# A retention and serf kernel on one core: k transposed on VectorE as q is, both from squares rearranged in DRAM

## Chip, cores and metric

The kernel runs on one core of one Trainium2 chip. The metric is the device time in microseconds (us) of one execution. The core has five engines that work at the same time, each through its own queue of instructions in order: TensorE (PE, with its weight loads as PEld), VectorE (DVE), ScalarE (ACT), GpSimd (POOL) and SyncE (SP), which here issues nearly all transfers. Sixteen DMA engines carry the transfers.

## The reference

Two blocks follow each other, all in float32. First comes retention, an attention without softmax: q, k and v have 8 batches of 8 heads with 576 positions of 64 values.

```python
scores = (1.0 / np.sqrt(D)) * np.matmul(q, k.transpose(0, 1, 3, 2))
gamma = 1.0 - 2.0 ** (-5.0 - np.arange(H))
rel = pos[:, None] - pos[None, :]
Dmat = np.where(rel >= 0, gamma[:, None, None] ** rel, 0.0)
x = np.matmul(scores * Dmat, v)          # then (B, H, S, D) -> (B*S, H*D): 4608 x 512
```

Then a feed-forward block with w_in (512 x 2048) and w_out (2048 x 512):

```python
h = x @ w_in
sp = np.maximum(h, 0.0) + np.log1p(np.exp(-np.abs(h)))
out = (h * erf(sp)) @ w_out
```

## The kernel before

**Attention by pieces.** A batch's 576 positions are cut into four pieces of 128 and one of 64, 40 pieces in all, numbered on through the batches. Each piece passes three stages. `transposes(i)` starts the loads of piece i + 3, weighs the values of piece i + 1 on GpSimd with decay powers gk (L276, in place in raw_v) and makes qT and kT, with two heads in the 128 partitions. `scores(i)` multiplies kT with qT (L311) and masks on VectorE (sT). `outputs(i)` forms o from sT and v (L323), adds the state of the pieces before (L334), makes the new state from kv (L346), and writes o, times its decay, into x (L376). The stages come in the fixed order transposes(i + 1), outputs(i), scores(i + 1). Because decay powers count from the start of the batch, the state is a plain sum: one copy on ScalarE (L358) or additions on VectorE; x takes one operation for each pair of heads, with a scalar gs by piece and a table gq.

**Two ways to transpose.** In batches 0 and 1, q and k go through TensorE against an identity (L296, into pt_q and pt_k) and are copied out by ScalarE (L297). VectorE transposes 32 x 32 squares only within themselves. From batch 2 on (`SQUARES = 2`), `load_squares(b)` fetches q of a whole batch in four transfers (L125) that bring every 32 x 32 square to the partitions where its transpose belongs, in runs of 32 values (128 B); VectorE then makes qT in one operation per piece (L299). k still goes through TensorE in all batches.

**Loads.** `load` fetches k and v (L115, four buffers each), and in the first two batches q (two buffers), each in two transfers with rows of 64 values (256 B). SP issues them in program order: an issue that waits for its buffer holds back all behind it.

**Feed-forward.** The 4608 positions are taken in 9 chunks of 512 (`TCH`), the hidden width in 4 groups. A `First` block multiplies x with w_in (L432) and a `Second` block the result with w_out (L511), each as seven products in a Strassen-like scheme, with sums on VectorE (the helper `tt`, L92) and copies, softplus and erf on ScalarE. In group 0 the steps of attention for later chunks are set between the products by hand: `attend(upto)` issues stages up to a mark, and `run(steps, rounds, stages)` calls it before each product. The operands of x are stored to DRAM (xd, L420) and read again for groups 1 to 3; partial outputs go to od (L567).

**Weights.** Each weight arrives as 64-bit words (wraw, three buffers, L200) and is rounded to float32 in steps: two operations on ScalarE (L217, L218), four on VectorE (L222 to L235), two on GpSimd (L236, L237), after which the next weight is fetched; four sums follow at the end of a set. `round_weights(n)` issues n such steps. In the first attention pieces, two steps follow each stage from the second on:

```python
    while done[0] < stages_for(TCH):
        attend(done[0] + 1)
        if done[0] >= 2:
            round_weights(2)
```

Of the kernel before, what the change touches and what calls it, by code (L numbers as in the profile page):

```python
# [11 lines left out]
FP32 = mybir.dt.float32  # L12
# [7 lines left out]
B, H, S, D = 8, 8, 576, 64  # L20
D_MODEL, D_FF = 512, 2048
NP = H // 2
NS = -(-S // P)
CONST_COLS = NS * H + NP * P + NS * NP + P

# [4 lines left out]
def decays():  # L32


    gamma = 1.0 - 2.0 ** (-5.0 - np.arange(H, dtype=np.float64))
    pairs = gamma.reshape(2, NP)
    t = np.arange(P)
    starts = np.arange(NS) * P
    gk = pairs.T.reshape(1, 1, H) ** -(starts[None, :, None] + t[:, None, None])
    row = pairs.repeat(D, axis=0)  # L40
    gq = row[:, :, None] ** t[None, None, :] / math.sqrt(D)
    gs = row[:, None, :] ** starts[None, :, None]
    tri = t[None, :] >= t[:, None]
    return np.concatenate([x.reshape(P, -1) for x in (gk, gq, gs, tri)], axis=1).astype(np.float32)


@with_exitstack
def kernel(
# [25 lines left out]
    dram = ctx.enter_context(tc.tile_pool(name="dram", bufs=n_ch, space=bass.MemoryType.DRAM))  # L74
    cpool = ctx.enter_context(tc.tile_pool(name="cpool", bufs=1))
    wpool = ctx.enter_context(tc.tile_pool(name="wpool", bufs=2))
    wraw = ctx.enter_context(tc.tile_pool(name="wraw", bufs=3))
    raw = ctx.enter_context(tc.tile_pool(name="raw", bufs=4))
    att = ctx.enter_context(tc.tile_pool(name="att", bufs=2))
    xpool = ctx.enter_context(tc.tile_pool(name="xpool", bufs=2))  # L80
# [15 lines left out]


    pieces = [(b, s0, min(P, S - s0)) for b in range(B) for s0 in range(0, S, P)]
    loaded = {i: {} for i in range(len(pieces))}


    SQUARES = 2
    SQ = 32

    def load(i, names="kv"):
        if i >= len(pieces):
            return
        b, s0, n = pieces[i]
        for name, src in (("q", q), ("k", k), ("v", v)):
            if name in names and not (name == "q" and b >= SQUARES):  # L110
                bufs = 2 if name == "q" else 4
                t = raw.tile([P, H, D], FP32, tag=name, name=f"raw_{name}", bufs=bufs)
                for e in range(2):
                    heads = src[b, e * NP : (e + 1) * NP, s0 : s0 + n, :]
                    nc.sync.dma_start(out=t[:n, e::2, :], in_=heads.rearrange("h p d -> p h d"))  # L115
                loaded[i][name] = t

    squares = {}

    def load_squares(b):  # L120
        if SQUARES <= b < B:
            t = squares[b] = raw.tile([P, NP, S // SQ, SQ], FP32, tag="q4", name="raw_q4", bufs=2)
            for part in range(P // SQ):
                e, d0 = part // 2, part % 2 * SQ
                nc.sync.dma_start(  # L125
                    out=t[part * SQ : (part + 1) * SQ].rearrange("r p a d -> r (p a) d"),
                    in_=q[b, e * NP : (e + 1) * NP, :, d0 : d0 + SQ].rearrange("p (a r) d -> r (p a) d", r=SQ),
                )

    load(0, "qkv")  # L130
    cst = cpool.tile([P, CONST_COLS], FP32, name="cst")
    nc.scalar.dma_start(out=cst, in_=consts)
    ends = [0]
    for m in (NS * H, NP * P, NS * NP, P):
        ends.append(ends[-1] + m)
    gk, gq, gs, tri = (cst[:, a:b] for a, b in zip(ends, ends[1:]))
    gk = gk.rearrange("p (s h) -> p s h", s=NS)
    gq = gq.rearrange("p (a i) -> p a i", a=NP)
    load(1, "qkv")
    load(2)  # L140


# [97 lines left out]
            if sums:  # L240
                yield from sums(*(w[:, i] for i in range(7)))

    for _ in range(3):
        load_weights()
    round_step = rounding()

# [23 lines left out]

    def weigh_values(i):

        if i < len(pieces):
            _, s0, n = pieces[i]
            t = loaded[i]["v"]
            nc.gpsimd.tensor_tensor(  # L276
                out=t[:n],
                in0=t[:n],
                in1=gk[:n, s0 // P, :].unsqueeze(2).to_broadcast([n, H, D]),
                op=ALU.mult,  # L280
            )

    def transposes(i):
        b, s0, n = pieces[i]
        t = live[i] = loaded.pop(i)
        load(i + 3)
        load(i + 2, "q")
        if s0 == 0:
            load_squares(b + 1)
        weigh_values(i + 1)  # L290
        for name in "qk":
            tT = t[name + "T"] = att.tile([P, NP, P], FP32, tag=name + "T", name=name + "T")
            if name in t:
                pt = ps_at.tile([P, NP, P], FP32, tag="at", name=f"pt_{name}")
                for p in range(NP):
                    nc.tensor.transpose(pt[:, p, :n], flat(t[name][:n, 2 * p : 2 * p + 2, :]), ident[:n, :n])  # L296
                nc.scalar.copy(out=tT[:, :, :n], in_=pt[:, :, :n])  # L297
            else:
                nc.vector.transpose(  # L299
                    out=tT[:, :, :n].rearrange("p a (s i) -> p a s i", i=SQ),  # L300
                    in_=squares[b][:, :, s0 // SQ : (s0 + n) // SQ, :],
                )

    def scores(i):
        n, t = pieces[i][2], live[i]
# [11 lines left out]
    def outputs(i):  # L317
# [24 lines left out]
        if s0 + n < S:  # L342
            kv = ps_at.tile([P, NP, D], FP32, tag="at", name="kv")
            for p in range(NP):
                for e in range(2):
                    nc.tensor.matmul(  # L346
                        kv[e * D : (e + 1) * D, p, :],
                        lhsT=t["k"][:n, 2 * p + e, :],
                        rhs=t["v"][:n, 2 * p + e, :],
                        start=(p == 0),  # L350
                        stop=(p == NP - 1),
                        skip_group_check=True,
                    )
            old = kept.get("state")
            if pieces[i + 1][2] > D:
                new = att.tile([P, NP, D], FP32, tag="state", name="state")
                if s0 == 0:
                    nc.scalar.copy(out=new, in_=kv)  # L358
                else:
                    tt(new, kv, old, ALU.add)  # L360
            else:
                new = states[b % 2]
                for r in heads:
                    tt(new[r, :, r], kv[r], old[r], ALU.add)
            kept["state"] = new
        t0 = b * S + s0
        while t0 < b * S + s0 + n:
            c = t0 // TCH
            if (0, c) not in x:
                x[0, c] = x_tile()  # L370
            m = min(b * S + s0 + n, (c + 1) * TCH) - t0
            a = t0 - b * S - s0
            at = slice(t0 - c * TCH, t0 - c * TCH + m)
            for p in range(NP):
                j = s0 // P * NP + p
                nc.vector.scalar_tensor_tensor(  # L376
                    out=x[0, c][:, p, at],
                    in0=o[:, p, a : a + m],
                    scalar=gs[:, j : j + 1],
                    in1=gq[:, p, a : a + m],  # L380
                    op0=ALU.mult,
                    op1=ALU.mult,
                )
            t0 += m

    stages = [(transposes, 0), (scores, 0)]
# [196 lines left out]
    weigh_values(0)  # L583
    while done[0] < stages_for(TCH):
        attend(done[0] + 1)
        if done[0] >= 2:
            round_weights(2)
    operands_x(0, 0)


# [2 lines left out]
    def run(steps, rounds=(), stages=1):  # L593

        for step, _ in enumerate(steps):
            attend(min(done[0] + stages, most[0]))
            if step in rounds:
                round_weights()

    run(firsts[0].first(), (0, 1), 2)  # L600
    run(firsts[0].middle(), (0, 1, 2), 2)
    run(firsts[0].last(), (0, 1), 2)
    firsts[0].erf()
    most[0] = stages_for(3 * TCH) - 1
    attend(stages_for(2 * TCH))
    operands_x(0, 1)
    round_weights(4)
    run(firsts[1].first(), (0, 1))
    firsts[0].multiply()
    round_weights(4)  # L610
    for b, nxt in zip(blocks[1:], blocks[2:] + [None]):
        n = order.index((b.g, b.c))
        if isinstance(b, First):
            most_g[0] = order[n - 1][0] + 1
            seconds[n - 1].begin()
            if n + 1 < n_s and order[n + 1][0] > 0:
                load_x(*order[n + 1])
            run(b.middle(), (0, 1))
            firsts[n - 1].sums()
            if n == 1:  # L620
                round_weights(9)
            run(seconds[n - 1].first(), (0, 1))
            run(b.last())
            most[0] = stages_for(min((n + 3) * TCH, n_tok)) - (n + 3 < n_ch)
        elif n + 2 < n_s:
            f = firsts[n + 1]
            for step, _ in enumerate(b.middle()):
                attend(min(done[0] + 1, most[0]))
                if step == 0:
                    f.erf()  # L630
            if n + 2 < n_ch:
                attend(stages_for((n + 3) * TCH))
            operands_x(*order[n + 2])
            run(nxt.first(), (0,))
            f.multiply()
            run(b.last(), (1,))
        elif n + 1 < n_s:
            firsts[n + 1].erf()
            seconds[n + 1].begin()
            run(b.middle())  # L640
            run(b.last())
            firsts[n + 1].multiply()
            firsts[n + 1].sums()
            run(nxt.first())
        else:
            run(b.middle())
            run(b.last())
# [30 lines left out]
```

## Time and profile before

| | |
|---|---|
| Median of three runs | 1090.24 us (1087.63 to 1090.39) |
| Profiled execution, its own time | 1091.13 us |
| Its span, first to last instruction | 1089.4 us |
| Mean granted TensorE clock | 0.987 |
| DMA moved | 178.60 MB in 170376 packets, 144448 of them under 512 B |
| Last copy of kT (piece 39) begins | 369.5 us |

A profile is one execution. The busy share of an engine is an average over stages with different limits, so the windows by stage say more than the page's sums. A line such as "A L1 <- B L2: us, times, longest" means that engine A stood idle before line 1 until line 2's work on B was done. A row of windows gives, for a stretch of the span, the busy time and number of instructions of PE, PEld, DVE, ACT and POOL, then the granted TensorE clock, the busy share of the DMA engines (packets can overlap, so it can pass 1) and the GB/s moved.

### The profile page before, as it was taken

Reading aid. Unit: us, or ns where it says so; the run is one execution under the profiler, and the core shown is the slowest. Engines: PE = TensorE matmul, PEld = TensorE weight load, DVE = VectorE, ACT = ScalarE, POOL = GpSimd, SP = SyncE. Lnnn points to the kernel's source line nnn. Section 1 sums busy time; section 2 is a strip of 40 time slices with the busy share of each in tenths; the row PEclk is TensorE's granted clock in tenths of the full one; section 3 lists DMA queues with packets and bytes.
Section 4 is the critical chain, followed back from the end, with each engine's and each line's share of the span. In section 5 each row is a group of like instructions: output and inputs, shape, how many; then the busy total and the mean of one; then the engine's idle time right before and its main releaser. Section 6 shows DMA issues by size and latency. Waiting matters only on the chain.

```text
span 1089.4 us, 15783 instructions
## 1 busy us (share of the span) xinstructions
PE 1051.2 (96%) x6472; PEld 901.3 (83%) x6472; DVE 625.4 (57%) x1074; ACT 397.2 (36%) x501; POOL 124.7 (11%) x110
## 2 busy tenths in 40 slices
PE   4899899999999999999999999999999999999996
PEld 3677788888888888888888888888888888888885
DVE  3738677577667663455555545555655445445444
ACT  2224322414324244433334444333344433333340
POOL 3313221121121000010001100110010000000000
PEclk8989899999999999999999999999999999999999
DMA  9787584665753253355555533555544333444432
GB/s 199 174 187 170 119 223 135 143 191 123 173 165 76 110 193 107 145 184 189 202 201 205 185 149 145 184 193 199 204 187 146 145 145 145 174 181 191 178 116 78
DMA packets 170376, 178.60 MB, mean 164 GB/s; under 512 B 144448, under 2 KB 144448, under 8 KB 162240
## 3 DMA queue, kind: packets, MB, share of 16 engines
q1 hardware_dynamic: 170160, 177.23, 51.5%
q8 instruction: 51, 0.84, 0.3%
q10 hardware_dynamic: 144, 0.36, 0.1%
q14 instruction: 21, 0.17, 0.1%
HBM read 123.30 MB, written 54.26 MB: 163 GB/s over the span
## 4 chain that ended last, share of the span: by engine, by line
PE 92%; DVE 3%; SPq 2%; DMA 2%; POOL 0%; issue 0%; DVEq 0%; POOLq 0%
PE a L511 23%; PE a L432 23%; PE g L511 12%; PE g L432 11%; PE e L432 6%; PE e L511 6%; PE o L323 3%; PE s L311 3%; PE o L334 3%; SPq L115 2%; PE kv L346 2%; PE pt_k L296 1%; DMA raw_q<-in_q_dram 1%; DVE t L92 1%; DMA wraw<-in_moe_w_in_dram 1%
## 5 line engine op out<-in xcount | busy, mean ns | idle before, releaser
L432 PE MATMUL a<-x,wa 128*128 128x256 f32 x1152 | 276.1, 383 | 0.0
L432 PEld LDWEIGHTS a<-x,wa 128*128 128x128 f32 x1152 | 217.4, 191 | 30.6 <-issue 0.4
L511 PE MATMUL a<-wb,s 128*128 128x256 f32 x864 | 205.9, 381 | 2.3 <-DVE o L92 2.3
L511 PEld LDWEIGHTS a<-wb,s 128*128 128x128 f32 x864 | 162.5, 190 | 26.1 <-DVE o L92 2.4
L92 DVE TENSOR_TENSOR t<-g,t 128x512 f32<-128x512 f32 x72 | 49.8, 691 | 159.6 <-ACT t L462 117.6
L432 PE MATMUL g<-x,wa 128*128 128x256 f32 x576 | 137.2, 381 | 0.0
L92 DVE TENSOR_TENSOR o<-a,o 128x512 f32<-128x512 f32 x108 | 74.3, 688 | 108.2 <-PE a L511 105.5
L432 PEld LDWEIGHTS g<-x,wa 128*128 128x128 f32 x576 | 108.2, 190 | 14.8
L236 POOL TENSOR_TENSOR wraw<-wraw 128x512 f32<-128x512 f32 x32 | 34.0, 1064 | 548.2 <-DVE wraw L235 312.6
L457 ACT COPY t<-a 128x512 f32<-128x512 f32 x36 | 21.1, 586 | 194.0 <-PE a L432 194.0
L92 DVE TENSOR_TENSOR t<-t,s 128x1024 f32<-128x1024 f32 x72 | 85.0, 1221 | 0.0
L474 ACT ACTIVATE s<-t 128x1024 f32<-128x1024 f32 x72 | 72.1, 1048 | 29.3 <-DVE t L92 29.3
L511 PE MATMUL e<-wb,t 128*128 128x256 f32 x288 | 69.7, 385 | 4.9 <-POOL wb L237 4.9
L468 ACT COPY t<-a 128x512 f32<-128x512 f32 x36 | 21.1, 586 | 143.1 <-PE a L432 143.1
L479 ACT ACTIVATE s<-s 128x1024 f32<-128x1024 f32 x72 | 72.1, 1049 | 0.4
L511 PE MATMUL a<-wb,t 128*128 128x256 f32 x288 | 68.6, 381 | 1.9 <-DVE t L92 1.9
L432 PE MATMUL e<-x,wa 128*128 128x256 f32 x288 | 70.2, 388 | 0.0
L511 PE MATMUL g<-wb,t 128*128 128x256 f32 x288 | 68.6, 381 | 0.0
L511 PE MATMUL g<-wb,s 128*128 128x256 f32 x288 | 68.5, 380 | 0.0
L276 POOL TENSOR_TENSOR raw_v<-raw_v,cst 128x512 f32<-128x512 f32 (+1 forms) x40 | 49.1, 1231 | 158.0 <-DMA raw_v<-in_v_dram 114.8
L511 PEld LDWEIGHTS e<-wb,t 128*128 128x128 f32 x288 | 54.6, 192 | 12.8 <-POOL wb L237 5.3
L511 PEld LDWEIGHTS a<-wb,t 128*128 128x128 f32 x288 | 54.1, 190 | 9.7 <-DVE t L92 2.3
(59 smaller groups left out, 1200.5 us busy)
## 6 DMA issues: line engine op xcount, KB each, us to landing
x<-xd SPq DMA_DIRECT2D x27, 1792.0 KB, 11.0
od<-o SPq DMA_DIRECT2D x54, 512.0 KB, 3.9
o<-od SPq DMA_DIRECT2D x27, 1024.0 KB, 7.3
xd<-x SPq DMA_DIRECT2D x9, 1792.0 KB, 6.5
out_dram<-o SPq DMA_DIRECT2D x18, 512.0 KB, 2.8
raw_k<-in_k_dram SPq DMA_DIRECT2D x64, 128.0 KB, 3.6
raw_v<-in_v_dram SPq DMA_DIRECT2D x64, 128.0 KB, 3.2
wraw<-in_moe_w_in_dram SPq DMA_DIRECT2D x32, 256.0 KB, 4.7
```

The lines of the kernel that those rows point to most:

```text
L92: nc.vector.tensor_tensor(out=out, in0=in0, in1=in1, op=op)
L115: nc.sync.dma_start(out=t[:n, e::2, :], in_=heads.rearrange("h p d -> p h d"))
L236: nc.gpsimd.tensor_tensor(out=r_f, in0=high_f, in1=r_f, op=ALU.mult)
L276: nc.gpsimd.tensor_tensor(out=t[:n], in0=t[:n], in1=gk[:n, s0 // P, :].unsqueeze(2).to_broadcast([n, H, D]), op=ALU.mult,)
L311: nc.tensor.matmul(ps[e][:n, p, :n], lhsT=t["kT"][r, p, :n], rhs=t["qT"][r, p, :n], start=True, stop=True)
L323: nc.tensor.matmul(o[e * D : (e + 1) * D, p, :n], lhsT=t["v"][:n, 2 * p + e, :], rhs=t["sT"][:n, e, p, :n], start=(p == 0), stop=(s0 == 0 ...
L334: nc.tensor.matmul(o[r, p, :n], lhsT=kept["state"][r, p, :], rhs=t["qT"][r, p, :n], start=False, stop=(p == NP - 1), skip_group_check=True,)
L346: nc.tensor.matmul(kv[e * D : (e + 1) * D, p, :], lhsT=t["k"][:n, 2 * p + e, :], rhs=t["v"][:n, 2 * p + e, :], start=(p == 0), stop=(p == ...
L432: nc.tensor.matmul(acc[:, j * TH : (j + 1) * TH], lhsT=weights["wa", self.g][:, a, d, j * P : (j + 1) * P], rhs=x[self.g, self.c][a][:, d, :],
L474: nc.scalar.activation(self.s[:, j], t, AF.Softplus)
L479: nc.scalar.activation(self.s[:, j], self.s[:, j], AF.Erf)
L511: nc.tensor.matmul(acc[:, tp, :], lhsT=left[:, j * TH + tp * P : j * TH + (tp + 1) * P], rhs=weights["wb", self.g][:, b, j, :], start=(sta ...
```

## The change

**k as q.** For batches from 2 on, `make_squares(b)` copies q and k of a whole batch within DRAM (sqq and sqk, four transfers each), in the order in which the squares are wanted. It is called at the second piece of the batch before. `load` then reads q4 and k4 of a piece from there in one transfer each, in runs of 128 values (512 B), beside k and v as before. VectorE makes both qT and kT.

**Decays.** The powers in gk and gq now count from the start of the piece. x takes one operation for all pairs of heads in a chunk. The state has to be scaled by gp = gamma to the power 128 at each piece: in the first piece on VectorE, later on GpSimd after a sum on VectorE.

**Rounding and buffers.** wraw has four buffers, q four. The first attention pieces issue three rounding steps after each stage from the sixth on; the first `First` block issues three steps after each product; bursts of four and nine later steps go away.

```diff
+    def make_squares(b):
+        if SQUARES <= b < B:
+            for name, src in (("q", q), ("k", k)):
+                t = squares[b, name] = dram.tile([P, NP, S // SQ, SQ], FP32, tag="sq" + name, name="sq" + name, bufs=B)
+                for part in range(P // SQ):
+                    e, d0 = part // 2, part % 2 * SQ
+                    nc.sync.dma_start(
+                        out=t[part * SQ : (part + 1) * SQ].rearrange("r p a d -> r (p a) d"),
+                        in_=src[b, e * NP : (e + 1) * NP, :, d0 : d0 + SQ].rearrange("p (a r) d -> r (p a) d", r=SQ),
+                    )
...
+        for name in "qk":
+            if b >= SQUARES:
+                t[name + "4"] = raw.tile([P, NP, P], FP32, tag="q" if name == "q" else "k4", name=f"raw_{name}4", bufs=4)
+                a = slice(s0 // SQ, (s0 + n) // SQ)
+                nc.sync.dma_start(
+                    out=t[name + "4"][:, :, :n].rearrange("p a (s d) -> p a s d", d=SQ), in_=squares[b, name][:, :, a, :]
+                )
...
         load(i + 3)
-        load(i + 2, "q")
-        if s0 == 0:
-            load_squares(b + 1)
+        if s0 == P:
+            make_squares(b + 1)
         weigh_values(i + 1)
         for name in "qk":
             tT = t[name + "T"] = att.tile([P, NP, P], FP32, tag=name + "T", name=name + "T")
-            if name in t:
+            if name + "4" in t:
+                nc.vector.transpose(out=tT[:, :, :n], in_=t[name + "4"][:, :, :n])
+            else:
...
-            old = kept.get("state")
-            if pieces[i + 1][2] > D:
-                new = att.tile([P, NP, D], FP32, tag="state", name="state")
-                if s0 == 0:
-                    nc.scalar.copy(out=new, in_=kv)
-                else:
-                    tt(new, kv, old, ALU.add)
-            else:
+            half = pieces[i + 1][2] == D
+            sums = kv
+            if s0 > 0:
+                sums = att.tile([P, NP, D], FP32, tag="sums", name="sums")
+                tt(sums, kv, kept["state"], ALU.add)
+            if half:
                 new = states[b % 2]
                 for r in heads:
-                    tt(new[r, :, r], kv[r], old[r], ALU.add)
+                    nc.gpsimd.tensor_tensor(out=new[r, :, r], in0=sums[r], in1=gp[r], op=ALU.mult)
+            else:
+                new = att.tile([P, NP, D], FP32, tag="state", name="state")
+                (nc.gpsimd if s0 > 0 else nc.vector).tensor_tensor(out=new, in0=sums, in1=gp, op=ALU.mult)
...
-            for p in range(NP):
-                j = s0 // P * NP + p
-                nc.vector.scalar_tensor_tensor(
-                    out=x[0, c][:, p, at],
-                    in0=o[:, p, a : a + m],
-                    scalar=gs[:, j : j + 1],
-                    in1=gq[:, p, a : a + m],
-                    op0=ALU.mult,
-                    op1=ALU.mult,
-                )
+            tt(x[0, c][:, :NP, at], o[:, :, a : a + m], gq[:, :, a : a + m], ALU.mult)
...
-        if done[0] >= 2:
-            round_weights(2)
+        if done[0] >= 6:
+            round_weights(3)
...
-    run(firsts[0].first(), (0, 1), 2)
-    run(firsts[0].middle(), (0, 1, 2), 2)
-    run(firsts[0].last(), (0, 1), 2)
+    run(firsts[0].first(), (3, 3), 2)
+    run(firsts[0].middle(), (3, 3, 3), 2)
+    run(firsts[0].last(), (3, 3), 2)
```

## The prediction

> **What bounds the kernel now.** I read the busy shares and the 40 slices first, then windows cut where the slices change, then what TensorE waited for.
>
> ```profile
> PE 1051.2 (96%) x6472; PEld 901.3 (83%) x6472; DVE 625.4 (57%) x1074; ACT 397.2 (36%) x501; POOL 124.7 (11%) x110
> ...
> PEclk8989899999999999999999999999999999999999
> DMA  9787584665753253355555533555544333444432
> ```
>
> TensorE is the bound nearly throughout; transfers are dense only in the first third, where attention runs. The windows give it in numbers (columns: PE, PEld, DVE, ACT, POOL busy, granted clock, DMA share, GB/s).
>
> ```profile
> 0.00:60.00 60.00, 38.93 (x372) 31.54 (x373) 31.66 (x64) 14.44 (x26) 19.07 (x22) 0.86 0.90 196
> 60.00:117.00 57.00, 48.84 (x457) 39.56 (x455) 36.98 (x82) 21.13 (x35) 18.64 (x13) 0.91 0.77 168
> 117.00:332.00 215.00, 215.00 (x1964) 175.96 (x1963) 149.30 (x303) 69.57 (x99) 41.71 (x37) 1.00 0.61 157
> 380.00:1062.00 682.00, 682.00 (x3162) 600.37 (x3162) 361.25 (x539) 273.76 (x321) 39.89 (x34) 1.00 0.47 171
> ```
>
> Until 117 us TensorE idles 29 us while DMA is at 0.8 to 0.9; from 117 to 1062 it never idles. All that the change touches ends by piece 39 at 370 us; the program after that is the same, so the forecast is when piece 39 comes. TensorE's waits, all before 117 us:
>
> ```profile
> PE pt_q L296 <- DMA raw_q<-in_q_dram: 11.3, 3, 5.2
> PE s L311 <- ACT kT L297: 6.4, 2, 5.7
> PE e L511 <- POOL wb L237: 4.9, 1, 4.9
> ```
>
> The rate of each kind of transfer is read from stretches that hold little else:
>
> ```profile
> 5.00:10.00 5.00, 4.02 (x24) 3.22 (x24) 0.00 (x0) 1.17 (x2) 1.04 (x1) 1.00 1.30 218
> 183.00:188.00 5.00, 5.00 (x59) 4.05 (x59) 4.30 (x7) 0.96 (x2) 0.06 (x1) 1.00 1.02 367
> 244.00:250.00 6.00, 6.00 (x60) 5.14 (x58) 5.96 (x9) 1.56 (x3) 1.04 (x1) 1.00 1.22 176
> ```
>
> Rows of 256 B (q, k, v by piece) run at about 215 GB/s, xd and od stores at 350, the squares of q (128 B pieces) at 175.
>
> **What the Trainium skill says.** "DMA: Bandwidth & Descriptors", section Specifications, asks for at least 512 B per transfer for line rate; the three rates agree. Its section "Why small descriptors are slow (HBM only)" puts the penalty on the HBM side; the squares now get an HBM end on both sides, and no row of the trace shows such a copy. "SBUF — State Buffer", section "Who interferes with whom", says that GpSimd and a VectorE operation with two SBUF inputs block each other; the trace agrees: a raw_v product that takes 1.04 us alone took 4.19 at 97.45, where t<-t,s ran.
>
> **The change part by part.** *K transposes, batches 2 to 7.* Each full piece had four pt_k matmuls, 0.44 us in the chain of waits, each half piece about 0.29: 24 x 0.44 + 6 x 0.29 = 12.3 us leave the bound engine; ScalarE loses 30 copies (0.59), and 30 pt_k accumulators come free, which nothing waited for after 117 us. VectorE gains 24 transposes of 0.70 and 6 of 0.43: 19.4 us. *Outputs.* 176 L376 operations (31.3 + 13.3 = 44.6 us) become 28 of about 0.69 and 16 of 0.42: 26 us. So VectorE's sum is unchanged, at 70% between 117 and 332, hidden by matmuls. *State.* VectorE keeps 32 operations of 0.42 for its 32 (eight that scale kv for eight copies that ScalarE made, and 8 sums instead of 16 half sums). GpSimd gains 16 products of 128x256 and 16 of 64x256: half of raw_v's 1.27, so 0.6 each, 20 us, at most 1 to 4 us each when blocked. The state is read a piece later, 9 us, which hides it; without that cover each piece would pay 1 to 4 us. Weigh_values and the rounding queue behind a product that waits for VectorE's sum; they too have a piece of slack. gk, gq and gp are built on the host: nothing.
>
> *Rounding and the first loads.* The count stays 24 steps before the first product, but none before the third transposes, so ScalarE's copies no longer stand behind the 16.7 us arrival of the first weights (kT, 6.4 us of TensorE wait, two thirds of it). q of piece 2 is loaded ahead of the weights (five of the 11.3). Three steps per product instead of one, and no burst of nine, finish wb before its use (4.9 us). The four weight buffers bring one 0.52 MB load forward ahead of piece 3, 1.8 us. Between nothing and 23 us can go; without more DMA I would take 11.
>
> *Transfers.* On SP's queue come, per batch from 2 on: four more DMAs of k squares; the q squares now write DRAM; two DMAs per piece that read 512 B runs back, behind a wait for the squares (q4, then k4), with that piece's k and v, then stores and weights, queued behind this wait. Prices: k and v of a piece 524 kB at 215 GB/s = 2.44 us; squares of one tensor 1.18 MB at 175 = 6.75; xd 1.84 MB 5.2; od half 1.5; one weight part 1.75 (300 GB/s). The 512 B runs lie between 215 and 350; from 11.7 ns (128 B) and 19 ns (256 B) per packet and engine I extrapolate 243 GB/s, so 2 x 262 kB = 2.16 us per piece. For the DRAM copy I keep 6.75 as the lower end, factor f = 1, and f = 2 as the upper (two HBM ends in turn); below 1 only if SBUF's side had set the old rate. I take f = 1.25, since each side's cost partly hides the other.
>
> Bill until piece 15 has landed: start 2; k, v 14.5 x 2.44 = 35.4; q 11; squares of batches 2 and 3, 27 f; read back 5.5 x 2.16 = 11.9; 12 weight parts 21; xd 2, 10.4; waits for squares to land, 2 x 2.5 = 5 (a load lands 2.2 us after issue at least); queue idle 10 (half of what shares of 0.90 and 0.77 leave in the first 117 us); landing 2. Sum 135.7 + 27(f - 1). Before, piece 15 had its kT at 148.1.
> Bill per batch from there: 4.5 x (2.44 + 2.16) = 20.7; squares 13.5 f; landing 2.5; xd and 2.25 od halves 8.6; 1.25 weight parts 2.2: 47.5 + 13.5(f - 1). Before, a batch took (332.8 - 148.1)/4 = 46.2; TensorE alone now asks 46.2 - 2.05 = 44.1. **DMA becomes the bound of the attention stage.**
> Piece 35, last first piece of a batch: at f = 1.25, 142.5 + 4 x 50.9 = 346 against 332.8: +13.2. After it no squares are made and TensorE saves its four last k transposes, 1.6. Net +11.6. The profiled execution took 1091.1 (span 1089.4 and 1.7 around it), 0.9 over the median 1090.2. So 1102.7 by its time, **1102** as median. TensorE's 12.3 us and the smoother start are eaten: the transposes wait for q4 and k4, and behind them in VectorE's queue stand the sums and the o adds that free TensorE's accumulators.
>
> **The rivals.** *The copy costs what the load did, f = 1:* 135.7 + 4 x 47.5 = 325.7, -7.1 - 1.6 = -8.7, about 1082. For it: reading 128 B pieces may set the rate alone. It is the other side; they part at f = 1.11, where the sum is zero. *TensorE stays the bound:* piece 15 at 148.1 - 11 - 2.5 = 134.6, then 4 x 44.1: 311, so -23, about 1067. That needs either f well under 1 or much faster read back; for it, a DMA share of 0.61 now leaves 18 us of a batch; against it, the change asks 6.75 + 9.7 + 2.5 = 19 at f = 1. *Read and write take turns, f = 2:* 162.7 + 4 x 61 = 406.7, +74 - 1.6: 1163. *The state product comes late* (GpSimd behind raw_v and rounding): 24 pieces x 1 us = +24, if covers fail; at 11% busy unlikely. *No effect:* the edits all appear in the order of instructions, so only by cancelling.
>
> **How the numbers follow.** Forecast (f 1.1 to 1.6) 0.49, from 1090 to 1130; f about 1 0.26, 1074 to 1090; TensorE bound 0.08; f above 1.6 0.12, to 1163; late state 0.05. A measurement here tells 0.3% (3.3 us). Faster takes the second case's larger part and the third: 0.28; same 0.08 from the seam of the first two; slower 0.64. Range 1072 to 1142; the likeliest case alone 1090 to 1130.
>
> **What would show it.** Right: DMA share near 1 from 60 to 340 us; VectorE's transposes waiting for raw_q or raw_k from sqq and sqk; TensorE idle at batch starts, with clock drops; squares of a batch taking 15 to 20 us together; batches at 50 us. The start (waits on qT, kT, wb) should shrink. Wrong: no TensorE waits after 117 us and batches of 44 us (then the 12.3 us count), or GpSimd's state among TensorE's releasers.

## The result and the profile after

The changed kernel takes 1091.95 us (1091.34 to 1092.91), against 1089.69 for the kernel before beside it: a ratio of 1.0025, interval [1.0007, 1.0042]. It is slower by about 2.3 us where 11.6 were forecast. The profiled execution has a span of 1091.1 us, 1.7 more than before.

Busy shares and slices of the changed kernel, from its page:

```profile
PE 1043.4 (96%) x6352; PEld 896.1 (82%) x6352; DVE 623.4 (57%) x972; ACT 379.4 (35%) x463; POOL 141.9 (13%) x142
...
PEclk9897999899998999999999999999999999999999
DMA  9799999999999453354555543545554333444432
```

TensorE has lost 7.8 us of work. The DMA row is full through the first third, where it stood mostly at 4 to 8, and PEclk now dips up to slice 13. The windows of the changed kernel, cut as before (columns: PE, PEld, DVE, ACT, POOL busy, granted clock, DMA share, GB/s):

```profile
0.00:60.00 60.00, 40.54 (x378) 33.33 (x380) 33.12 (x52) 16.12 (x28) 22.18 (x26) 0.86 0.95 212
60.00:117.00 57.00, 47.43 (x450) 39.25 (x451) 37.15 (x64) 18.01 (x29) 21.39 (x20) 0.88 0.96 202
117.00:332.00 215.00, 209.48 (x1888) 171.23 (x1886) 149.79 (x253) 56.44 (x71) 44.59 (x50) 0.98 1.00 220
380.00:1062.00 682.00, 682.00 (x3177) 600.10 (x3176) 359.89 (x535) 273.15 (x320) 39.82 (x34) 1.00 0.47 171
```

From 117 to 332 us the DMA share is 1.00 (it was 0.61), and TensorE idles where it never did. What TensorE waited for, first up to 117 us (three lines), then after it (two lines):

```profile
PE pt_q L299 <- DMA raw_q<-in_q_dram: 10.9, 2, 5.7
PE o L321 <- DVE sT L90: 9.6, 3, 9.1
PE o L321 <- issue: 7.5, 2, 4.0
...
PE o L332 <- POOL state L360: 7.6, 2, 4.5
PE s L309 <- DVE kT L295: 2.4, 1, 2.4
```

Of the waits of before, that for kT has fallen from 6.4 to 0.7 us and that for wb is gone. New are one stall of 9.1 us that ends with sT, 7.5 us before two products of o for which the list names no releaser ("issue"), and 10.0 us after 117, most of it for the state on GpSimd. The two unnamed waits end at 37.89 and 52.52 us, each about 0.5 to 0.8 us after VectorE began the mask of that piece (37.11 and 52.02), which stood there behind rounding steps, and behind sums for wa and x: by these times they too are waits for sT.

In the table a piece is dated by the start of its first mask (sT) on VectorE, from the timeline of the run's one profiled execution; "pace" is pieces 15 to 35, a quarter of it, so one batch.

| kernel | piece 2 | 3 | 8 | 9 | 15 | 35 | 39 | pace |
|---|---|---|---|---|---|---|---|---|
| before | 32.0 | 38.3 | 84.1 | 94.7 | 154.4 | 339.0 | 376.9 | 46.1 |
| after | 22.2 | 37.1 | 79.5 | 98.4 | 150.8 | 342.8 | 378.6 | 48.0 |
| e1_k_by_pe | 22.1 | 37.9 | 81.6 | 93.3 | 145.1 | 329.6 | 367.2 | 46.1 |
| e2_q_direct | 22.1 | 34.7 | 79.6 | 96.3 | 148.6 | 328.6 | 364.3 | 45.0 |
| e3_weigh_late | 21.5 | 36.7 | 80.8 | 91.0 | 142.5 | 332.4 | 368.1 | 47.5 |
| e4_k_copied_twice | 22.1 | 37.5 | 82.4 | 104.3 | 165.8 | 377.4 | 413.2 | 52.9 |
| e6_v_first | 22.0 | 37.6 | 82.6 | 95.9 | 148.3 | 332.8 | 368.5 | 46.1 |
| e11_squares_early | 21.7 | 37.9 | 81.2 | 98.6 | 150.6 | 336.7 | 372.4 | 46.5 |
| e12_q_direct_v_first | 22.1 | 35.5 | 79.6 | 93.2 | 144.8 | 320.0 | 355.7 | 43.8 |

**What stands behind a late v.** The chain of waits of the changed kernel around its longest stall (start, us, what):

```profile
87.58 4.60 DMA raw_v<-in_v_dram
...
92.37 1.01 POOL raw_v L281
93.38 1.01 POOL wraw L240
...
94.46 1.29 POOL wb L241
...
95.77 1.15 DVE wb L90 x2
...
98.47 0.34 DVE sT L90
...
98.86 1.45 PE o L321 x16
```

No operation in it is slow. The values of a piece land at 92.2; GpSimd, in order, has held the rounding of a weight behind them; VectorE, in order, has a sum of that weight ahead of the mask of a piece that needs neither; TensorE waits for the mask. In SP's queue k's read back for this batch went out at 85.21, and v only at 87.03. The whole order is seen in the next batch (start, us, issues):

```profile
118.12 6.55 SPq L110 DMA_DIRECT2D sqq<-in_q_dram  x4
124.71 7.94 SPq L110 DMA_DIRECT2D sqk<-in_k_dram  x4
132.76 1.47 SPq L204 DMA_DIRECT2D wraw<-in_moe_w_out_dram  x1
134.34 0.57 SPq L124 DMA_DIRECT2D raw_q<-sqq  x1
136.16 0.57 SPq L124 DMA_DIRECT2D raw_k<-sqk  x1
136.78 1.16 SPq L132 DMA_DIRECT2D raw_k<-in_k_dram  x2
137.99 1.06 SPq L132 DMA_DIRECT2D raw_v<-in_v_dram  x2
```

The read back of k's squares may be issued only when all four copies have landed, at 136.16, and k and v, which need no squares, are issued after it. The wait itself is small in the list of SP's waits, 8.5 us in eight times from 117 to 340; the experiments ask what it holds back.

### The profile page after: what moved, and what is told of

It reads as the page before. It is cut to its first block, busy times and chain, and to the rows that moved or that the text cites. A ratio compares the mean times of both kernels' runs of the same rounds, so it can differ in the third digit from the quotient of the medians.

```text
span 1091.1 us, 15454 instructions
## 1 busy us (share of the span) xinstructions
PE 1043.4 (96%) x6352; PEld 896.1 (82%) x6352; DVE 623.4 (57%) x972; ACT 379.4 (35%) x463; POOL 141.9 (13%) x142
## 4 chain that ended last, share of the span: by engine, by line
PE 91%; DMA 2%; DVE 2%; SPq 1%; POOL 1%; issue 1%; ACT 0%; POOLq 0%; DVEq 0%; ACTq 0%
PE a L501 23%; PE a L422 23%; PE g L422 12%; PE g L501 11%; PE e L501 6%; PE e L422 5%; PE s L309 3%; PE o L321 3%; PE o L332 3%; PE kv L344 2%; SPq L132 1%; DMA raw_v<-in_v_dram 1%; DMA raw_q<-in_q_dram 1%; DMA wraw<-in_moe_w_in_dram 1%; DVE t L90 0%
## 5 line engine op out<-in xcount | busy, mean ns | idle before, releaser
L422 PE MATMUL g<-x,wa 128*128 128x256 f32 x576 | 140.2, 387 | 0.0
L422 PEld LDWEIGHTS g<-x,wa 128*128 128x128 f32 x576 | 110.6, 194 | 15.8
L447 ACT COPY t<-a 128x512 f32<-128x512 f32 x36 | 21.1, 585 | 201.7 <-PE a L422 201.7
L458 ACT COPY t<-a 128x512 f32<-128x512 f32 x36 | 21.1, 586 | 160.3 <-PE a L422 160.3
L281 POOL TENSOR_TENSOR raw_v<-raw_v,cst 128x512 f32<-128x512 f32 (+1 forms) x40 | 45.7, 1142 | 190.7 <-DMA raw_v<-in_v_dram 135.0
L452 ACT COPY t<-a 128x512 f32<-128x512 f32 x36 | 21.1, 585 | 128.1 <-PE a L422 128.1
L90 DVE TENSOR_TENSOR sT<-s,cst 128x512 f32<-128x512 f32 (+1 forms) x80 | 47.0, 629 | 27.4 <-PE s L309 27.2
```

The source lines that it names most:

```text
L90: nc.vector.tensor_tensor(out=out, in0=in0, in1=in1, op=op)
L281: nc.gpsimd.tensor_tensor(out=t[:n], in0=t[:n], in1=gk[:n, :].unsqueeze(2).to_broadcast([n, H, D]), op=ALU.mult)
L422: nc.tensor.matmul(acc[:, j * TH : (j + 1) * TH], lhsT=weights["wa", self.g][:, a, d, j * P : (j + 1) * P], rhs=x[self.g, self.c][a][:, d, :],
L447: nc.scalar.copy(out=self.t1[:, 1], in_=self.a)
```

## The experiments

The four factors by themselves came first: k's way, q's way, the place of GpSimd's products, and the bytes.

**e1_k_by_pe: q through DRAM, k by TensorE.**

```diff
-            for name, src in (("q", q), ("k", k)):
+            for name, src in (("q", q),):
...
-        for name in "qk":
+        for name in "q":
```

> The kernel after, with k transposed by TensorE in all batches again and no squares of k; q still goes through DRAM. Queue theory (the DMA queue, full from 60 to 340 us, sets the pace of the attention stage): a batch loses 7.4 us of k squares and 4.9 us of reading back, so it needs some 34 us of transfers against 46.2 us of TensorE; no TensorE waits after 117 us, batches of 46 us, time 1086 to 1092, about the kernel before. Order theory (GpSimd's raw_v product, waiting for a late v, holds up the state product and the rounding behind it): v still stands behind the squares of q, so half of the waits on the state product stay, 1092 to 1096. Start theory (what is lost is lost in the first 117 us by the moved rounding): +4 us at piece 10 as in the kernel after, and then nothing, 1094 or more.

Measured 1081.21, ratio 0.9924 [0.9909, 0.9939]: 8 us faster than before, some 11 faster than the changed kernel, and faster than all three theories had it. Pace 46.1, as before; the gain over before, 9.4 us, is there by piece 15: it is the gain of the start, which the theories had left out. From 117 to 332 us:

```profile
117.00:332.00 215.00, 215.00 (x1948) 176.17 (x1947) 140.63 (x229) 64.76 (x92) 52.47 (x53) 1.00 0.75 187
```

With k's 1.18 MB of squares and its read back gone, the DMA share is 0.75 and TensorE never idles. So moving k costs what the rest of the change brings, and a little more.

**e2_q_direct: q's squares straight to SBUF, as before; k's through DRAM.** To make room, q and k4 share three buffers, wraw has three, and the state is scaled in place.

```diff
-                t = squares[b, name] = dram.tile([P, NP, S // SQ, SQ], FP32, tag="sq" + name, name="sq" + name, bufs=B)
+                pool, bufs = (raw, 2) if name == "q" else (dram, B)
+                t = squares[b, name] = pool.tile([P, NP, S // SQ, SQ], FP32, tag="sq" + name, name="sq" + name, bufs=bufs)
...
-        for name in "qk":
+        for name in "k":
```

> The kernel after, with the squares of q fetched straight into SBUF a batch at a time as in the kernel before, k still through DRAM. To make room, k4 shares three buffers with q, three weight buffers instead of four, one padded state instead of two, and the state is scaled in place. Queue theory: a batch loses 4.9 us of reading q back, 46.6 - 4.9 = 41.7 us of transfers against 44.1 us of TensorE, so TensorE is the bound again and its 2.05 us per batch count: batches of 44 to 45 us, time 1078 to 1084. Order theory: v still stands behind two sets of squares, so the waits on the state product stay, 1087 to 1091.

Measured 1079.97, 0.9911 [0.9897, 0.9926]; pace 45.0. Fewer bytes and one read back fewer per piece are worth 12 us, with the changed buffers, whose share was not separated. SP still waited 15.1 us for sqk between 117 and 340, and a stall of 7.0 us before 117 stayed.

**e3_weigh_late: raw_v's product behind the state's on GpSimd.**

```diff
-        weigh_values(i + 1)
+        if i == 0:
+            weigh_values(1)
...
             kept["state"] = new
+        weigh_values(i + 2)
```

> The kernel after, with each raw_v product issued on GpSimd behind the state product of the outputs stage instead of ahead of it; every transfer stays as it is. Queue theory: the waits only change their name (kT or qT for want of k4, raw_v itself), time 1088 to 1093. Order theory: the waits of o on the state product (7.6 us after 117 us) and the stall of 9 us at 90 us go, time 1076 to 1082.

Measured 1083.26, 0.9941 [0.9927, 0.9956]. The stall of 9.1 us at piece 9 is gone and piece 15 comes 8.3 us sooner than in the changed kernel. The pace hardly moves, and TensorE's wait after 117 us only changes its name:

```profile
PE s L310 <- DVE kT L296: 11.8, 3, 6.8
```

**e4_k_copied_twice: a second copy of k's squares that nobody reads.**

```diff
-            for name, src in (("q", q), ("k", k)):
+            for name, src in (("q", q), ("k", k), ("2", k)):
```

> The kernel after, with the squares of k copied a second time into a DRAM tile that nothing reads: 4 more transfers per batch, six batches. Queue theory: each copy adds its 7.4 us to a queue that is already full, +35 to +50 us, about 1135. If the queue had slack and only the order mattered: v is late by 7.4 us more at each batch start only, +5 to +20 us.

Measured 1130.02, 1.0373 [1.0356, 1.039]: six copies cost 38 us, 6.35 each on the average. In the table they cost 7.5 us each up to piece 15 and 4.9 a batch from there to piece 35. TensorE's waits after 117 us:

```profile
PE o L332 <- POOL state L360: 32.1, 5, 7.4
```

So the changed kernel has little room for another copy. But the copy also stands ahead of the next k and v in SP's queue, so this run does not tell the bytes from the order. Nor is 6.35 us the time of the copy itself: waits and a slower mean clock (0.966 against 0.978) are in it.

**e5_q_direct_late: e2_q_direct and e3_weigh_late together.** On top of e2_q_direct:

```diff
-        weigh_values(i + 1)
+        if i == 0:
+            weigh_values(1)
...
+        weigh_values(i + 2)
```

> The two edits that won together: q squares straight into SBUF (as in e2_q_direct) and the raw_v product behind the state product (as in e3_weigh_late). Queue theory with the order as a second cause: transfers ask about 42 us a batch, TensorE 44.1, and nothing is queued behind a late v, so TensorE is the bound from 117 us: batches of 44.1 to 44.6 us from piece 15 to 35, 4 times 2 us better than the kernel before, on top of the 9 to 12 us that e1 and e3 were ahead at piece 15: 1068 to 1073. If the two edits take away the same stall: 1078 to 1081.

Measured 1080.73, 0.9918 [0.99, 0.9937]: nothing over e2_q_direct. Piece 15 is 3.2 us sooner (145.4), but the pace is 46.9. SP's queue in one batch, and the DMA engines in the window at its end:

```profile
215.86 7.72 SPq L111 DMA_DIRECT2D sqk<-in_k_dram  x4
228.51 0.57 SPq L125 DMA_DIRECT2D raw_k<-sqk  x1
229.17 1.12 SPq L133 DMA_DIRECT2D raw_k<-in_k_dram  x2
230.39 1.26 SPq L133 DMA_DIRECT2D raw_v<-in_v_dram  x2
```

```profile
225.00:230.00 5.00, 5.00 (x50) 4.03 (x48) 0.75 (x2) 1.00 (x2) 0.34 (x1) 1.00 0.35 51
```

From 223.6 to 228.5 SP waits for the squares to land with nothing else issued; the DMA engines fall to a share of 0.35, and v stands behind. Exchanging products on GpSimd only chooses who passes the lateness on. That moved the suspicion from GpSimd to SP's order.

**e6_v_first: v and k issued ahead of the read back, all else as changed.**

```diff
+        for name, src in (("q", q), ("k", k), ("v", v)) if b < SQUARES else (("v", v), ("k", k)):
...
         for name in "qk":
             if b >= SQUARES:
...
-        for name, src in (("q", q), ("k", k), ("v", v)):
```

> The kernel after, with v and k of a piece loaded ahead of its q4 and k4 (so ahead of the wait for the squares), GpSimd's order unchanged. Order theory: what stalled GpSimd is that v is issued behind the squares' landing, so v first cures it as weighing late did: 1081 to 1086, with the waits moved to kT. Queue theory alone: q4 and k4 come 2.4 us later instead, and they are what VectorE waits for: no gain, 1090 to 1094.

Measured 1083.94, 0.9952 [0.9936, 0.9967]: 8 us from order alone, with the same bytes. Pace 46.1; the state wait falls from 7.6 to 4.4 us.

**e7_decays_alone and e8_rounding_alone: the kernel before with one part of the change.** The first takes the tables, weigh_values, the state and the write of x from the changed kernel; the second its rounding steps (`done[0] >= 6` with three steps, three per product, no bursts), with q's two and wraw's three buffers as before. Their main lines:

```diff
-                    tt(new[r, :, r], kv[r], old[r], ALU.add)
+                    nc.gpsimd.tensor_tensor(out=new[r, :, r], in0=sums[r], in1=gp[r], op=ALU.mult)
```

```diff
-        if done[0] >= 2:
-            round_weights(2)
+        if done[0] >= 6:
+            round_weights(3)
...
-    run(firsts[0].first(), (0, 1), 2)
+    run(firsts[0].first(), (3, 3), 2)
```

> The kernel before with the decays of the kernel after alone: one x operation per chunk, the state scaled on GpSimd (in place, one padded state). By the prediction's sums VectorE saves 18.6 us and GpSimd gains 20 us, both hidden behind TensorE: within 2 us of the kernel before, 1087 to 1091. If the state product was late by itself: +5 to +24 us. If VectorE's x operations were on the path of the first 117 us: -3 to -6 us.

> The kernel before with the rounding schedule of the kernel after alone (three weight buffers, loads as before). Prediction: the wait of 4.9 us of wb and the slow clock after it go, and two thirds of the 6.4 us of kT: 1079 to 1084. Start theory turned round (what the earlier rounding takes away comes back as waits for q of pieces 2 and 3): only the 4.9 us and a little clock, 1083 to 1087.

The decays: 0.9996 [0.9986, 1.0005], no cost. The rounding: 1.0016 [1.0007, 1.0025], no gain either, where both of its theories had one. TensorE's waits up to 130 us in e8_rounding_alone:

```profile
PE pt_q L296 <- DMA raw_q<-in_q_dram: 17.7, 3, 9.5
PE o L323 <- DVE sT L92: 5.8, 4, 2.6
```

The waits for kT (6.4) and wb (4.9) went, but the wait for q grew from 11.3 to 17.7: earlier pieces only arrive sooner at a q that is loaded behind weights. So the start's gain is not the rounding's alone. That it needs q's two further buffers and its earlier load with it is likely, but these were not tried by themselves.

**e11_squares_early: the squares issued one piece sooner.**

```diff
-        if s0 == P:
+        if s0 == 0:
             make_squares(b + 1)
```

> The changed kernel with one line altered: the squares of the next batch are made while the first piece of a batch is transposed, not the second. The bytes, the DMAs and their count stay; between the squares' issue and the first read back of them now stands a whole piece's loads. Theory A (what costs is that SP's queue waits for the squares to land with v and k standing behind the wait): the wait on sqq and sqk (10.4 us in ten stretches) shrinks below 4 us, TensorE's state wait goes, the pace from piece 15 to piece 35 falls from 48.0 to 45.5 us a batch and the time to about 1080. Theory B (the bytes alone fill the queue): pace 47.5 to 48, time within 3 us of 1092, and the waits only move to another piece.

Measured 1088.07, 0.9983 [0.9973, 0.9994], between the theories. SP's wait for squares is gone from the list, the pace falls by 1.5 us, but v still lands late, now as plain traffic behind the squares (before the longest wait of TensorE it is issued at 178.82 and lands at 182.50, after squares issued from 159.04 on):

```profile
PE o L332 <- POOL state L363: 9.4, 5, 5.4
```

This reads as if of what e6_v_first gains, part were the wait and part v's place ahead of the read back's bytes. At the start the stall of 9.1 us is gone, yet piece 9 comes no sooner (98.6): the squares now stand ahead of the last q that TensorE transposes, that of piece 9. TensorE waits 2.7 us for it, runs at a mean clock of 0.67 from 80 to 90 us, and waits 2.8 us for sT.

**e12_q_direct_v_first and e13_q_direct_early: e2_q_direct with either remedy.** On top of e2_q_direct, the first line in e12_q_direct_v_first (ahead of k4), the second in e13_q_direct_early:

```diff
+        for name, src in (("q", q), ("k", k), ("v", v)) if b < SQUARES else (("v", v), ("k", k)):
...
-        if s0 == P:
+        if s0 == 0:
```

> q squares straight to SBUF and k through DRAM, as in e2_q_direct, and v and k of a piece issued ahead of its k4. Theory A (late v behind the landing wait holds the state and the rounding): each of the two was worth about 9 us by itself; together the transfers fit (a batch asks 2.16 us less for each of 4.5 pieces) and v is early, so TensorE becomes the bound: 44.1 to 44.6 us a batch, about 1070 to 1074, and no TensorE wait of over 1 us after 117 us. Theory B (the 5 us that e2_q_direct still loses are lost before 117 us, at the start): 1078 to 1080, pace 45.0 as there.

> q squares straight to SBUF, k through DRAM, and the squares made a piece earlier (as in e11_squares_early), v and k behind k4 as in the changed kernel. Theory A: nothing on SP waits for squares to land (under 2 us), pace 44.1 to 44.6, 1070 to 1074. Theory B: as e2_q_direct, 1078 to 1080. If here the time is lower than in e12_q_direct_v_first, the k4 wait itself costs, not only what stands behind it.

e12_q_direct_v_first: 1071.01, 0.9826 [0.9808, 0.9843], 19 us less than before. Its window, and all TensorE's waits from 117 to 1060 us, both in the feed-forward block:

```profile
117.00:332.00 215.00, 215.00 (x1952) 176.62 (x1952) 156.83 (x266) 58.52 (x73) 49.89 (x54) 1.00 1.04 218
```

```profile
PE a L507 <- DVE t L90: 1.9, 1, 1.9
PE a L507 <- DVE o L90: 1.5, 2, 0.8
```

TensorE is the bound again at 43.8 us a batch. e13_q_direct_early: 1075.46, 0.9874 [0.985, 0.9898], with the same pace of 43.8; a time between its two theories. It loses 5 us at the start, nearly all from piece 7 to piece 8 (72.8 to 85.3, against 71.2 to 79.6): as in e11_squares_early q of piece 9 is issued behind the squares, at 78.80, and TensorE waits 2.6 us for it and is slower afterwards. With q's bytes gone from the way, either remedy suffices for the pace. Order and bytes add up:

| | v, k behind the read back | v, k ahead of it |
|---|---|---|
| q through DRAM | 1.0025 (after) | 0.9952 (e6_v_first) |
| q straight to SBUF | 0.9911 (e2_q_direct) | 0.9826 (e12_q_direct_v_first) |

Each step is worth 7 to 9 thousandths in a row and 11 to 13 in a column.

**e16_two_weights: q of piece 3 ahead of the third weight.**

```diff
-    for _ in range(3):
+    for _ in range(2):
         load_weights()
...
         load(i + 3)
+        if i == 0:
+            load_weights()
```

> e12_q_direct_v_first with the first loads in another order: two of the three first weight parts ahead of piece 3, the third behind it, so that q of piece 3 lands about 2 us earlier. After 117 us e12_q_direct_v_first has TensorE without a wait; what is left to gain is the 22 us of waits before. Theory A (the start is a matter of order alone: q of piece 3 stands behind the weights): the waits for raw_q (9.5 us) fall to about 7, and piece 15 and the time come 2 us sooner, about 1069. Theory B (the start is bound by the bytes: what q gains, the weights and then the rounding and the first products lose): piece 3 comes 2 us sooner, piece 10 and piece 15 within 1 us of e12_q_direct_v_first, time within 1.5 us of 1071.

Measured 1070.18, 0.9817 [0.9804, 0.983]; the interval overlaps that of e12_q_direct_v_first. The waits for q fall from 9.5 to 5.3 us and piece 3 comes 1.1 us sooner, but piece 15 only 0.2: theory B. The remaining 22 us of waits before 117 us are not a matter of this order; what else would shorten them was not tried.

## Why the prediction was wrong

Its sum by parts, against the two profiled executions:

| step | predicted | measured |
|---|---|---|
| up to piece 15 | -5.6 | -3.6 |
| four batches, piece 15 to 35 | +18.8 | +7.5 |
| after piece 35 | -1.6 | -2.2 |
| sum | +11.6 | +1.7 |

**The step that failed is "I take f = 1.25".** The load into SBUF from which the prediction took its price ran at 176 GB/s (244 to 250 us of the kernel before). In the changed kernel the same 128 B pieces moved within DRAM at 157, 168 and 154 GB/s:

```profile
120.00:125.00 5.00, 5.00 (x56) 4.08 (x53) 2.42 (x5) 4.64 (x5) 1.61 (x2) 1.00 1.00 157
125.00:130.00 5.00, 5.00 (x49) 4.04 (x48) 3.18 (x5) 0.00 (x0) 0.00 (x0) 1.00 1.15 168
130.00:135.00 5.00, 5.00 (x47) 4.17 (x48) 4.24 (x8) 0.59 (x1) 0.61 (x1) 1.00 1.07 154
```

Against their mean f is 1.10. By the traces' records of single packets, from a batch's first 128 B packet to its last, q into SBUF took 7.1 to 8.1 us in the kernel before (mean 7.5), and q and k within DRAM together 14.8 to 16.3 in the changed one (mean 15.5, so 7.8 each): f is 1.03. Within one kernel, e12_q_direct_v_first, k's copy in DRAM was not the slower of the two, though q's stands first in the queue, behind other loads; the list of its transfers from 117 to 332 us gives the median time to landing of an issue of 288 KB:

```profile
sqk<-in_k_dram SPq DMA_DIRECT2D x20, 288.0 KB, 5.5
sqq<-in_q_dram SPq DMA_DIRECT2D x17, 288.0 KB, 6.6
```

So f lies at about 1.03 to 1.10, just below the break-even of 1.11. The prediction leaned on the Trainium skill, "DMA: Bandwidth & Descriptors", section "Why small descriptors are slow (HBM only)", but a toll for each HBM end was its own step: the section's two mechanisms are overheads of each packet and each descriptor. The runs show no second toll beyond this tenth. As the bill moves by 27 + 4 x 13.5 = 81 us with f, 1.25 was 12 to 18 us too much; with the f measured the bill forecasts a total of 1084 to 1090.

It then gives 47.9 to 48.9 us a batch, and 48.0 was measured. This agreement is in part luck: in e6_v_first the same transfers, in another order, ran at 46.1, which is near the bill without its 2.5 us for landing (45.4 to 46.4).

**A second step failed the other way, by 6 to 8 us up to piece 15.** With the f measured the bill puts piece 15 at -11.6 to -9.7, and it came at -3.6. The prediction did say that k and v are queued behind the wait for the squares, but it put their lateness at nothing: the work queued on GpSimd was to have "a piece of slack". It named q4 and k4 as what TensorE would wait for. Of TensorE's waits after 117 us 2.4 end with kT, but 7.6 with the state, and the stall of 9.1 us before stands behind v as well: GpSimd's and VectorE's queues carried the lateness of v to work that has nothing to do with v. Three different edits that spare v, or the whole queue, bring piece 15 to -9.4 (e1_k_by_pe), -6.1 (e6_v_first) and -11.9 us (e3_weigh_late).

So the measured +1.7 is the forecast of +11.6, less 12 to 18 us for f, plus 6 to 8 by piece 15, and 0 to 4 less for the rest. That it lies so near to zero is a balance of terms that have nothing to do with each other; it does not mean that the change does little.

**The late state** was given 0.05, argued from GpSimd's 11% of busy time. It is what ends the longest waits after 117 us: 7.6 us in all here, 32.1 in e4_k_copied_twice. The share of busy time said nothing on it, since GpSimd was waiting, not working; its chain at 185 to 194 us in the changed kernel:

```profile
185.79 3.58 DMA raw_v<-in_v_dram
...
189.52 1.04 POOL raw_v L281
190.56 0.57 POOL state L360
...
191.20 0.62 POOL state L360
...
191.87 1.97 PE o L332 x8
```

And such a stall costs more than its length. Windows of the changed kernel right after it:

```profile
192.00:196.00 4.00, 4.00 (x14) 3.55 (x15) 0.43 (x1) 0.00 (x0) 2.30 (x3) 0.50 1.06 398
196.00:200.00 4.00, 4.00 (x27) 2.98 (x26) 1.99 (x4) 0.58 (x1) 1.01 (x1) 0.79 1.08 264
```

The clock is 0.50 for four microseconds and 0.79 for four more, so by estimate 2.8 us (4 x 0.50 + 4 x 0.21) on top of the 3.07 that TensorE stood idle. The Trainium skill, "TensorE: Matmul & The Clock Gate", section "What's actually happening", has the clock fall to half after an idle window of about 3.4 us. Here shorter waits did it, and the measurement decides: this one of 3.07 us, and also the wait of 2.4 us for kT, after which the clock is 0.50 from 245.5 to 248.9 us.

**What was right.** *Transfers become the bound of the attention stage*: yes, but not by all of the 48.0 us a batch. The squares of a batch take 18 us from the first issue (118.12) to the read back (136.16), as forecast; and with v first in both, taking q's way through DRAM out brings the pace from 46.1 (e6_v_first) to 43.8 (e12_q_direct_v_first). By this the transfers ask about 46 us a batch, and the order in the queue adds the rest. *K transposes*: e12_q_direct_v_first has a pace of 43.8 against 46.1, 2.3 us a batch where the bill had 2.05. *VectorE's sum unchanged*: 149.79 us against 149.30 from 117 to 332. *Decays at nothing*: e7_decays_alone. *The start*: the waits for kT and wb went as said, and piece 2 came 9.9 us sooner, but piece 3 only 1.2. TensorE waits 5.7 us for q of piece 3, which is issued behind eight transfers of weights, and then about 4 us for its mask, which stands behind three rounding steps on VectorE. That the gain is of about the size put down (11) is seen only without the stall: 9.4 us in e1_k_by_pe.

The rival in which TensorE stays the bound, 1067, was right in its number for a kernel that this change is not: e12_q_direct_v_first, at 1071.

## What to carry to other kernels

When a transfer that waits for another transfer is put into a queue, list what stands behind it in that queue, and what stands behind each of those in the in-order queues that consume them; here 8 us came from issuing v and k, which need no squares, ahead of the read back. A transfer that nobody reads tells in one run whether a queue has room left; it is not the price of the transfer, since it delays what stands behind it as well. And price a new kind of transfer from both sides with a run before resting a sign on it: the whole forecast turned on f, and its break-even of 1.11 lay just above the measured 1.03 to 1.10.

## What the runs showed of the hardware

Copying 128 B pieces from DRAM to DRAM took on average 3 to 10% longer than loading them into SBUF: 7.8 us per tensor of a batch against 7.5, or a mean of 160 GB/s against 176. TensorE's clock fell to 0.50 after waits of 3.07 and of 2.4 us. And a DMA share of 1 does not prove the bound: the changed kernel has 1.00 and waits, e12_q_direct_v_first has 1.04 at 218 GB/s and TensorE never waits for it from 117 to 332 us. What TensorE and SP wait for tells the two apart, not the share.
